# First batch's attention in 64x64 tiles, and one lying layout for keys, queries and values of batches 0 and 1

## The chip, the cores and the metric

The kernel runs on one core of a Trainium2 chip. Five engines work side by side, each through its own row of instructions in order: TensorE (PE; its weight loads PEld apart), VectorE (DVE), ScalarE (ACT), GpSimd (POOL) and SyncE (SP). They wait for each other through semaphores. Sixteen DMA engines move data; POOL and SP issue the transfers. The metric is the device time of one execution in microseconds (us); lower is better.

## What is computed

Longformer attention (a window of 32 to both sides and 8 global positions) over 8 batches of 8 heads, 576 positions and 64 dimensions, and behind it a two-layer product with a snake activation on the 4608 rows of 512.

```python
scores = scale * np.matmul(q, k.transpose(0, 1, 3, 2))
mask = np.abs(pos[:, None] - pos[None, :]) <= window
mask = mask | is_global[:, None] | is_global[None, :]
attn = softmax(where(mask, scores, -1e9))
x = (attn @ v) as rows of 512           # 4608 x 512
h = x @ w_in                             # 512 x 2048
s = np.sin(alpha * h)
out = (h + s * s / (alpha + 1e-09)) @ w_out
```

## The kernel before

The loop runs over batches. For batch b the phase *attention(b)* makes scores, masks, denominators and numerators for four head pairs (hp) and leaves xT, the normalised result, transposed. *gemm1(b)* multiplies xT by w_in in 16 groups (nt) of 128 columns: eight matmuls, a sine on ScalarE (sb), its square on ScalarE or VectorE (s), and one operation on VectorE that writes H2. *gemm2(b)* multiplies H2 by w_out in blocks of 128 rows, 16 matmuls of 512 columns each. It is not a phase of its own: it waits as a generator, and `fill(n)` puts n of its matmuls where the author of the order set them (START, FIRST, SECOND, PER_GROUP), in attention(b+1) and gemm1(b+1). So in the first attention and first gemm1 nothing can be filled in; `warm(z, n)` issues n matmuls without use there. The order of instructions on each engine is the order of the code: nothing is scheduled, and an engine in front of a wait holds all behind it.

Positions are dealt in 12 tiles of 48 keys, even and odd positions apart (y = 0 and 1), and 8 global keys follow each tile. For batches 1 to 7 scores come in 64x64 tiles: head t of a pair on partitions t\*64 and on, and two key tiles (the two halves of the sequence) share one score tile of 128 partitions by 2\*360 columns. The first batch has a function of its own, `attention_first`: it keeps keys and values of a pair block-diagonal in KD and VD, 128x128, so that these must be cleared first, and its score tile is 128x480. Its mask MASK lies by tiles, and is moved to MASKT by DMA for the batches behind it.

Set-up: POOL loads keys and queries of batch 0 in four pieces of 288 KB (each half of the heads of k, then of q), casting to bf16. TensorE transposes them (L625), and ScalarE and VectorE copy them from PSUM into KD and QX (L641, L646), the first half ahead of the attention and the second in it (`second_half`). Values of batch 0 come in 16 loads of runs of 64 elements, 128 bytes in bf16 (L397). Batch 1's values are cast into DRAM (L343, vd) and read back by SP (L418, VX). Batch 1's keys and queries are loaded lying (48 rows of 3072) and turned by TensorE in three thirds within gemm1(0) (L733, placed by L741 and L747). SP gathers the rows of the 8 global positions of all batches, eight small transfers each for k, q and v (L518); `turn_kq` transposes them in gemm1(0) at group 4 (L773, then the casts L777 to kTg and qTg).

From batch 2 on keys and queries are cast into DRAM (kd, qd) by POOL and transposed by DMA from there (kt, qt, L353, on SP, `turn_qk`); `place` copies them into KX and QX on VectorE in eight pieces (L369, L362). Values are cast into DRAM (vd) and read in four transfers on SP (`load_v`, L418). POOL's casts are paced: before batch 2's cast of values POOL waits for qt of batch 2 (`pace`, L347).

## Time and profile before

| | us |
|---|---|
| runs, median (lowest to highest of 3) | 351.45 (350.79 to 351.58) |
| profiled execution | 351.02 |
| its span in the trace | 349.2 |
| TensorE busy in the span | 314.1 (90%) |
| VectorE busy | 274.7 (79%) |
| ScalarE busy | 285.7 (82%) |
| first scores of batch 0 | 16.04 |
| first sine of batch 0 | 36.12 |
| first scores of batch 1 | 59.92 |
| first sine of batch 1 | 78.13 |
| first scores of batch 2 | 98.75 |

How to read it: a line of the timeline has the start and the length in us, the engine, the line of the program, the operation, what it writes and reads, and in brackets how long its engine was idle before and what ended that. Lengths of neighbours overlap a little, since the engines are pipelined; the distance of two starts is what one takes of the engine. The stretch from the first scores of one batch to those of the next is one round; after batch 2 the rounds repeat.

### The profile page before, as it was taken

The page shows a single profiled execution, that of the slowest core. Times are in us where ns is not written, and L with a number is a line of the kernel's source. Part 1 is how long each engine was busy: PE and PEld are TensorE (multiplying, and loading weights), DVE is VectorE, ACT ScalarE, POOL GpSimd, SP SyncE. Part 2 cuts the span into 40 slices and gives each one's busy share as a digit, 9 for nine tenths or more (in the row PEclk, how much of TensorE's full clock was granted, in tenths as well). Part 3 has the DMA queues.
Part 4 walks back from the last instruction along what each step waited for, and adds up shares of the span by engine and source line. Part 5 has one row for each costly group of instructions (what it writes and reads, how often), then busy time and mean ns, then how long its engine had stood idle before and what let it go on. Part 6 is the DMA issues. An engine that isn't in the chain of part 4 may idle for free.

```text
span 349.2 us, 10913 instructions
## 1 busy us (share of the span) xinstructions
PE 314.1 (90%) x4425; PEld 206.7 (59%) x4484; DVE 274.7 (79%) x537; ACT 285.7 (82%) x428; POOL 60.9 (17%) x93
## 2 busy tenths in 40 slices
PE   1578799899899999999999999999989999999994
PEld 1557576466655675567656765577557755665543
DVE  6786778878879788887798787978797788788940
ACT  6797688898988888989898889989898888888721
POOL 7966130023004000400012000400000000002600
PEclk9999899999999999999999999999999999999999
DMA  7999999689997948399529962791824111010232
GB/s 114 110 132 159 184 212 232 116 155 187 190 171 140 196 71 190 76 204 150 108 65 188 200 107 64 152 191 45 171 65 95 30 33 66 3 30 2 76 92 67
DMA packets 87762, 42.25 MB, mean 121 GB/s; under 512 B 72378, under 2 KB 82362, under 8 KB 87322
## 3 DMA queue, kind: packets, MB, share of 16 engines
q0 software_dynamic: 44944, 18.52, 44.1%
q1 hardware_dynamic: 42762, 22.98, 30.7%
q8 instruction: 36, 0.59, 0.8%
q14 instruction: 20, 0.16, 0.2%
HBM read 41.97 MB, written 20.77 MB: 180 GB/s over the span
## 4 chain that ended last, share of the span: by engine, by line
PE 67%; DMA 6%; DVE 5%; issue 4%; ACT 2%; SPq 1%; POOL 0%; DVEq 0%; ACTq 0%
PE zo L1270 30%; PE zn L1176 12%; PE zr L1176 9%; PE zd L1176 8%; PE ring L976 3%; DMA vd<-in_v_dram 3%; PE zn L1014 2%; DVE H L1221 2%; PE zd L1014 2%; DMA VD<-vd 2%; DMA qt<-qd 2%; DVE QX L362 2%; SPq L353 1%; PE zd L1314 1%; PE zd L1270 1%
## 5 line engine op out<-in xcount | busy, mean ns | idle before, releaser
L1270 PE MATMUL zo<-w_out,H 128*128 128x512 bf16 (+1 forms) x517 | 134.1, 376 | 5.9 <-issue 5.2
L1176 PEld LDWEIGHTS <-w_in 128*128 128x128 bf16 x1024 | 100.3, 98 | 48.6 <-issue 13.2
L1270 PEld LDWEIGHTS <-H 128*128 128x128 bf16 x592 | 53.6, 98 | 45.8 <-DMA VX<-vd 0.3
L1176 PE MATMUL zn<-xT,w_in 128*128 128x288 bf16 (+1 forms) x384 | 57.0, 287 | 5.7 <-DVE GN L801 2.7
L1176 PE MATMUL zr<-xT,w_in 128*128 128x288 bf16 x320 | 48.7, 291 | 1.2 <-DVE H L1221 1.2
L1176 PE MATMUL zd<-xT,w_in 128*128 128x288 bf16 x320 | 46.9, 290 | 0.2
L1221 DVE SCALAR_TENSOR_TENSOR H<-s,recipT,zn 128x576 bf16<-128x576 bf16 (+1 forms) x48 | 39.4, 821 | 9.1 <-ACT s L1218 5.7
L1215 ACT ACTIVATE sb<-zn,alphaT 128x576 bf16<-128x576 f32 (+1 forms) x48 | 35.6, 742 | 12.4 <-PE zn L1176 12.1
L1218 ACT ACTIVATE s<-sb 128x576 bf16<-128x576 bf16 (+1 forms) x58 | 40.0, 689 | 1.8
L1221 DVE SCALAR_TENSOR_TENSOR H<-s,recipT,zd 128x576 bf16<-128x576 bf16 (+1 forms) x40 | 32.9, 822 | 9.3 <-ACT s L1218 6.5
L1220 DVE TENSOR_TENSOR s<-sb 128x576 bf16<-128x576 bf16 (+1 forms) x70 | 32.1, 459 | 10.0 <-ACT sb L1215 9.8
L985 ACT ACTIVATE E<-ring 128x720 bf16<-128x720 f32 x42 | 32.8, 781 | 7.5 <-PE ring L976 6.8
L1221 DVE SCALAR_TENSOR_TENSOR H<-s,recipT,zr 128x576 bf16<-128x576 bf16 (+1 forms) x40 | 32.9, 822 | 6.2 <-ACT s L1218 4.6
L1215 ACT ACTIVATE sb<-zr,alphaT 128x576 bf16<-128x576 f32 (+1 forms) x40 | 29.7, 742 | 7.6 <-PE zr L1176 7.6
L986 DVE TENSOR_TENSOR E<-E,MASKT 128x720 bf16<-128x720 bf16 x56 | 29.4, 529 | 8.0 <-ACT E L985 6.3
L1215 ACT ACTIVATE sb<-zd,alphaT 128x576 bf16<-128x576 f32 (+1 forms) x40 | 29.5, 738 | 5.8 <-PE zd L1176 5.7
L1277 ACT COPY osb<-zo 128x512 f32<-128x512 f32 (+1 forms) x36 | 20.9, 581 | 10.7 <-PE zo L1270 7.0
L824 ACT ACTIVATE R<-L,shift 128x576 f32<-128x576 f32 x32 | 25.1, 784 | 0.5
L1260 POOL COPY H<-H 128x11 bf16 (+1 forms) x16 | 7.2, 452 | 98.7 <-DVE H L1221 97.9
L347 POOL COPY seen<-xT 1x1 bf16<-1x1 bf16 x4 | 1.9, 479 | 125.5 <-DVE GN L801 125.5
L1035 DVE TENSOR_TENSOR xT<-zn,R 128x576 bf16<-128x576 f32 x21 | 15.8, 753 | 1.1 <-PE zn L1014 0.9
L343 POOL DMA_DIRECT2D vd<-in_v_dram x7 | 16.3, 2333 | 0.1
(187 smaller groups left out, 376.9 us busy)
## 6 DMA issues: line engine op xcount, KB each, us to landing
vd<-in_v_dram POOLq DMA_DIRECT2D x7, 576.0 KB, 16.3
kd<-in_k_dram POOLq DMA_DIRECT2D x6, 576.0 KB, 8.2
qd<-in_q_dram POOLq DMA_DIRECT2D x6, 576.0 KB, 10.0
VX<-vd SPq DMA_DIRECT2D x16, 168.0 KB
w_in<-in_moe_w_in_dram POOLq DMA_DIRECT2D x4, 512.0 KB, 9.2
w_out<-in_moe_w_out_dram POOLq DMA_DIRECT2D x4, 512.0 KB, 24.4
VD<-vd SPq DMA_DIRECT2D x12, 168.0 KB
out_dram<-osb SPq DMA_DIRECT2D x7, 256.0 KB
```

What stands on the lines that cost most here:

```text
L343: nc.gpsimd.dma_start(out=cast[b, "vd"][:], in_=v[b].rearrange("h s d -> s h d"))
L824: nc.scalar.activation(out=R[:], in_=L[:], func=AF.Exp, scale=-1.0, bias=shift[:, 0:1])
L985: nc.scalar.activation(out=Eg, in_=z[:, :, 0 : G3 * WCOL], func=AF.Exp, scale=scale)
L986: nc.vector.tensor_tensor(out=Eg, in0=Eg, in1=MASKT[:, None, G3 * g : G3 * (g + 1), :].rearrange("p o m c -> p o (m c)").to_broadcast([P, ...
L1035: nc.vector.tensor_tensor(out=xT[:, hp, 0:S].rearrange("p (k m c) -> p k m c", k=4, c=KT), in0=tokens(nd(hp, 0)), in1=Rs[hp][:], op=ALU.mult,)
L1176: nc.tensor.matmul(out=h_part, lhsT=w_in[:, c, nt * P : (nt + 1) * P], rhs=xT[:, c, lo:hi], start=(c == 0), stop=(c == CT - 1), skip_group ...
L1215: nc.scalar.activation(out=sb[:, 0:W], in_=h, func=AF.Sin, scale=alphaT[:, nt : nt + 1])
L1218: nc.scalar.activation(out=s2[:, 0:W], in_=sb[:, 0:W], func=AF.Square)
L1220: nc.vector.tensor_tensor(out=s2[:, 0:W], in0=sb[:, 0:W], in1=sb[:, 0:W], op=ALU.mult)
L1221: nc.vector.scalar_tensor_tensor(out=H2[:, nt, r0 : r0 + W], in0=s2[:, 0:W], scalar=recipT[:, nt : nt + 1], in1=h, op0=ALU.mult, op1=ALU.add,)
L1270: nc.tensor.matmul(out=ops[:, cols], lhsT=H2[:, nt, blk * P : (blk + 1) * P], rhs=w_out[:, nt, cols], start=(nt == 0), stop=(nt == NT - 1) ...
L1277: nc.scalar.copy(out=osb[:, cols], in_=ops[:, cols])
```

## The change

`attention_first` goes. Batch 0 runs through the same function as the others, in 64x64 tiles; where there is nothing to fill in, `warm` puts two or three matmuls a head pair. KD, VD, OB and MASK go with their clearing, and the mask is made in MASKT at once.

Keys and queries of batches 0 and 1 are loaded in one lying layout, in pieces by head parity (t), all of k ahead of all of q. `turn_lying` and `place_lying` turn and place them: batch 0 wholly in the set-up, in 192 transposes instead of 96 and in copies of 128 partitions; batch 1 in gemm1(0), at groups 4, 7 and 10 instead of 2, 6 and 9. Values of batches 0 and 1 are loaded by pairs of neighbouring positions, in runs of 128 elements (256 bytes in bf16) into VF; VectorE then moves the odd rows to partitions 32 further on (`odd_rows`) and copies the two tiles at the border of the halves (`edge_tiles`, VE). Batch 1's values thus don't go through DRAM any more. Global values of batch 0 are repeated through a small DRAM tile (vgd).

Other places: the order of the loads on POOL and of the gathers on SP; `turn_kq` at group 12 of gemm1(0), behind that group's matmuls; the turn of batch 2's keys and queries behind attention(1) instead of at its second head pair; their placing wholly in gemm1(1); gemm2(0) takes the first eight groups of two blocks first.

```diff
-    def load_v0(hps):
-        for hp in hps:
-            for t in range(2):
-                for y in range(2):
-                    r = t * D + y * 24
-                    nc.gpsimd.dma_start(
-                        out=VD[r : r + 24, hp, :, t * D : t * D + D],
-                        in_=v[0, 2 * hp + t].rearrange("(i a y) d -> y a i d", a=24, y=2)[y],
-                    )
+    def load_v_lying(b, hs):
+        for h in hs:
+            for half in range(2):
+                nc.gpsimd.dma_start(
+                    out=VF[b][half * D : half * D + NH, :, h].rearrange("p m y d -> p m (y d)"),
+                    in_=v[b, h].rearrange("(n m a y) d -> n a m (y d)", n=2, a=NH, y=2)[half],
+                )
+    def odd_rows(b, hs, copy):
+        for half in range(2):
+            r = half * D
+            copy(out=VF[b][r + 32 : r + 32 + NH, :, hs, 0], in_=VF[b][r : r + NH, :, hs, 1])
+    def edge_tiles(b, hs, copy):
+        for half in range(2):
+            r, m = (1 - half) * D, half * (NT6 - 1)
+            for y in range(2):
+                o = half * D + y * 32
+                copy(out=VE[b][o : o + NH, hs], in_=VF[b][r : r + NH, m, hs, y])
...
-    load_v0((0,))
+    load_v_lying(0, range(0, 4))
     load_w_in((0,))
-    load_v0((1, 2))
+    load_v_lying(0, range(4, 8))
     load_w_in((1,))
-    load_v0((3,))
-    load_lying(0)
     load_lying(1)
     load_w_in((2, 3))
-    cast_v(1)
-    load_w_out()
+    load_w_out((0, 1))
+    load_v_lying(1, range(H))
+    load_w_out((2, 3))
+    gather(k, gk, range(3))
+    bounce_vg0()
+    gather(k, gk, range(3, 6))
     load_vg0()
+    gather(k, gk, range(6, NG))
     gather(q, gq)
+    gather(v, gv)
...
+    def turn_lying(b, w, third, z):
+        rows = slice(D * w, D * w + NI)
+        for r in range(R16):
+            for t in range(2):
+                nc.tensor.transpose(
+                    out=z[t * D : (t + 1) * D, r * NI : (r + 1) * NI], in_=lie[b][rows, t, third * R16 + r],
+                    identity=identb[rows, rows],
+                )
+    for w in (1, 0):
+        for third in range(3):
+            turn_lying(0, w, third, lain[w][third])
...
+    warm(idle, 5)
...
-        if b == 0:
-            return attention_first(beside)
...
-            fill(SECOND[hp])
+            spare_or(SECOND[hp] if b else 2)
...
+    TURNED, PLACED, GLOBALS = (4, 7, 10), (5, 8, 11), 12
-            if b == 1 and nt in (10, 12):
-                for which, t, y in PLACES[nt - 6 : nt - 4]:
+            if b == 1 and nt in (3, 6, 9, 12):
+                for which, t, y in PLACES[2 * nt // 3 - 2 : 2 * nt // 3]:
                     place(2, which, t, y, nc.vector.tensor_copy)
-            if b == 0 and nt == 4:
-                turn_kq()
...
+            if b == 0 and nt == GLOBALS:
+                turn_kq()
...
+            if b_att < 2 and at in ((0, 2) if b_att == 0 else (0,)):
+                hs = slice(at * H // 4, H // 2 + at * H // 4) if b_att == 0 else slice(0, H)
+                odd_rows(b_att, hs, nc.vector.tensor_copy)
+                edge_tiles(b_att, hs, nc.vector.tensor_copy)
...
-            if b_moe == 0 and at == 1:
+            if b_moe == 0 and at == NHP:
                 turn_qk(2)
```

How instructions move, at two places. VectorE in the first attention, before: masks of the first head pair (E, MASK), then the queries of the second half (QX), then the second pair.

```order
L851 TENSOR_TENSOR E<-E,MASK 128x480 x3
L646 COPY QX_95<-zo_124 64x2x6x2x12 x4
L646 COPY QX_95<-zo_125 64x2x6x2x12 x4
L851 TENSOR_TENSOR E<-E,MASK 128x480 x3
L801 TENSOR_REDUCE GD<-zd 128x2x4
```

The same place after; VF holds the values, VE the edge tiles.

```order
L862 TENSOR_TENSOR E<-E,MASKT 128x2x360 x2
L402 COPY VF_91<-VF_91 24x6x4x64 x2
L409 COPY VE_93<-VF_91 24x256 x4
L862 TENSOR_TENSOR E<-E,MASKT 128x2x360 x2
L794 TENSOR_REDUCE GD<-zd 128x2x4
```

The copies of queries have left the attention, and copies of values stand where they stood (and once more behind the masks of the third pair).

SP from the second head pair of batch 1's attention on, before: kt and qt are the DMA transposes of batch 2, LC stores logarithms, out_dram stores output blocks.

```order
L819 DMA LC<-L 2x576
L353 DMA_TRANSPOSE kt<-kd 128x2304
L353 DMA_TRANSPOSE qt<-qd 128x2304
L819 DMA LC<-L 2x576
L1303 DMA out_dram<-osb 16x512
L1303 DMA out_dram<-osb 112x512
L819 DMA LC<-L 2x576 x2
L1303 DMA out_dram<-osb 32x512
L1303 DMA out_dram<-osb 96x512
L418 DMA VD<-vd 24x7x512 x4
```

And after, from the second output block on:

```order
L1170 DMA out_dram<-osb 112x512
L812 DMA LC<-L 2x576 x2
L1170 DMA out_dram<-osb 32x512
L1170 DMA out_dram<-osb 96x512
L352 DMA_TRANSPOSE kt<-kd 128x2304
L352 DMA_TRANSPOSE qt<-qd 128x2304
L440 DMA VF_91<-vd 24x7x512 x4
```

The two transposes stand behind the stores of the third block, and directly ahead of the reads of batch 2's values.

More of the change, by code (lines that the diff above doesn't have):

```diff
@@ L432, in load_w_in, with load_w_out @@
             )
[L434 to L435 removed]
+    def load_w_out(gs):
+        for g in gs:
             nc.gpsimd.dma_start(
@@ L614 @@
     )
     small = tc.alloc_tile_pool(name="small", bufs=1, space=PSUM)
-    both = small.tile([P, 512], DT.float32, name="pg")
+    both, idle = [small.tile([P, 512], DT.float32, name=name) for name in ("pg", "idle")]
     act, dve = nc.scalar.copy, nc.vector.tensor_copy
-    part = {}
-    def turn_part(w, half, z):
-        part[w, half] = z
-        rows = slice(D * half, D * half + HK)
-        for a in range(NH):
-            nc.tensor.transpose(
-                out=z[a // 12][:, a % 12], in_=nat[w][rows, a * P : (a + 1) * P], identity=identb[rows, rows]
-            )
@@ L1281, in gemm2 @@
         full = slice(0, DM)
-        if b == B - 1:
-            for blk in (lo, lo + 1):
-                yield from products(blk, bank(blk), range(SOON), full)
+        ahead = {0: NT // 2, B - 1: SOON}.get(b, 0)
+        for blk in (lo, lo + 1):
+            yield from products(blk, bank(blk), range(ahead), full)
         for blk in range(lo, hi):
```

475 lines of the change are left out of this document (167 added, 308 removed).

## The prediction

> **What bounds the kernel now.** I read the span by stages first. The columns are the stretch, its length, the busy time of TensorE, its weight loads, VectorE, ScalarE and GpSimd with their instructions, the granted clock, the DMA share and GB/s. The stages: first attention, first matrix product of batch 0, attention of batch 1, first product of batch 1.
>
> ```profile
> 16.04:36.12 20.08, 16.20 (x182) 13.38 (x182) 15.09 (x44) 16.09 (x29) 13.88 (x19) 1.00 1.22 151
> 36.12:59.92 23.80, 20.66 (x320) 14.43 (x318) 17.74 (x27) 18.49 (x30) 4.08 (x7) 0.93 1.43 213
> 59.92:78.13 18.21, 16.84 (x394) 10.27 (x399) 14.25 (x30) 16.30 (x25) 2.12 (x3) 1.00 0.78 141
> 78.13:98.75 20.62, 18.61 (x130) 12.58 (x130) 18.00 (x30) 17.40 (x27) 3.53 (x4) 1.00 1.50 181
> ```
>
> From 60 us on TensorE is busy 90% or more, because a second product always has matmuls to put in a gap. Before that no engine is full: in the first two rows TensorE, VectorE and ScalarE are each busy three quarters of the time and wait in turn. The change can only win in these 44 us; what follows 98.75 keeps its order. So the sum runs to the first scores of batch 2, at 98.75. The timeline of the set-up and first attention says why its engines wait.
>
> ```profile
> 3.23 0.52 POOL L473 DMA_DIRECT2D H<-in_q_dram  x1
> 6.42 1.14 PE L625 MATMUL zn<-identb,H 48*128 48x48 bf16 x24 [6.42 <-DMA H<-in_k_dram]
> 16.04 0.96 PE L843 MATMUL ring<-QX,KD 128*128 128x120 bf16 x8 [1.17 <-ACT alphaT L709]
> 18.38 3.21 ACT L641 COPY KD<-zn 64x288 bf16<-64x288 bf16 x8
> 18.95 3.74 DVE L646 COPY QX<-zo 64x288 bf16<-64x288 bf16 x8
> 22.23 0.56 PE L843 MATMUL ring<-QX,KD 128*128 128x120 bf16 x4 [2.00 <-ACT E L850]
> 24.52 0.63 PE L576 MATMUL zo<-ones 128*128 128x512 bf16 x1
> 28.82 0.38 PE L576 MATMUL zo<-ones 128*128 128x512 bf16 x1
> 36.12 0.74 ACT L1215 ACTIVATE sb<-zn,alphaT 128x576 bf16<-128x576 f32 x1
> H<-in_q_dram POOLq DMA_DIRECT2D x1, 288.0 KB, 8.7
> ```
>
> ScalarE and VectorE spend 3.21 and 3.74 us inside the attention on the second half of keys and queries, and TensorE waits 2.00 for it. The same 512-column matmul takes 0.63 at 24.5 and 0.38 at 28.8: TensorE runs at a lower speed until about 28 us. The next stage holds one stall.
>
> ```profile
> 37.22 0.70 PE L733 MATMUL zo<-identb,H 48*64 48x48 bf16 x64
> 40.25 0.95 DVE L741 COPY KX<-zo 128x768 bf16<-128x768 bf16 x1
> 41.25 0.96 PE L773 MATMUL zo<-idf,H 64*128 64x64 f32 x8 [1.78 <-DVE KX L741]
> 42.15 2.10 PE L1176 MATMUL zr<-xT,w_in 128*128 128x288 bf16 x8
> 42.25 0.42 DVE L777 CAST kTg<-zo 128x256 bf16<-128x256 f32 x1 [0.33 <-PE zo L773]
> 44.28 0.74 ACT L1215 ACTIVATE sb<-zr,alphaT 128x576 bf16<-128x576 f32 x1 [3.32 <-PE zr L1176]
> 42.00:43.00 1.00, 1.00 (x6) 0.61 (x6) 0.75 (x2) 0.00 (x0) 0.00 (x0) 0.50 2.38 172
> ```
>
> The transposes of the global rows (L773) wait for a key copy, TensorE idles 1.78, its clock falls to 0.50, and ScalarE idles 3.32.
>
> **Term 1: the first scores, 16.04 to 17.5 (+1.5).** The loads are still four of 288 KB, but each turn now takes both pieces of its tensor, and the queries come last: the fourth load, issued at 3.23, lands 8.7 later, at 11.9. Then 96 query transposes stand on TensorE. Bounds: 0.70/64 = 11 ns each, over four quarters of the array (1.05 us), and 1.14/24 = 48 ns each (4.6). I take 30 ns (2.9), nearer to L625, which runs at this place and speed. Five warming matmuls follow, 0.38 to 0.63 each: 1.9 to 3.2, I take 2.5. With 0.2 for the global rows that makes 17.5; the bounds give 15.1 to 19.9. The copies on ScalarE and VectorE lie beside this. The memsets and clears that go saved no wait: the loads ended last.
>
> **Term 2: the first attention, 20.1 to 15.2 (-4.9).** The shapes are now those of batch 1.
>
> ```profile
> 59.92 0.35 PE L976 MATMUL ring<-QX,KX 64*64 64x88 bf16 x14
> 61.25 0.77 ACT L985 ACTIVATE E<-ring 128x720 bf16<-128x720 f32 x1
> 62.05 1.20 DVE L986 TENSOR_TENSOR E<-E,MASKT 128x720 bf16<-128x720 bf16 x2 [0.55 <-ACT E L985]
> 65.31 0.68 ACT L817 ACTIVATE L<-zd 128x576 f32<-128x576 f32 x1
> 66.03 0.23 DVE L801 TENSOR_REDUCE GD<-zd 128x8 f32<-128x64 f32 x1 [0.62 <-ACT L L817]
> 66.51 0.81 ACT L824 ACTIVATE R<-L,shift 128x576 f32<-128x576 f32 x1
> 68.26 0.75 DVE L1035 TENSOR_TENSOR xT<-zn,R 128x576 bf16<-128x576 f32 x1
> 68.38 0.49 PE L1014 MATMUL zd<-E,ones 56*64 56x88 bf16 x28
> 73.96 0.91 DVE L369 COPY KD<-kt 64x1152 bf16<-64x1152 bf16 x2
> 77.29 1.91 DVE L369 COPY KD<-kt 64x1152 bf16<-64x1152 bf16 x2
> ```
>
> ScalarE: eight exponentials at 0.77, four logarithms at 0.68, four inverses at 0.81: 12.1. VectorE: eight masks at 0.60, four normalisations at 0.75, eight sums at 0.23: 9.6. New on VectorE are four copies of odd rows (1536 elements a partition) and eight of edge tiles (256). The trace has no such copy; the nearest is 1152 elements in 0.455. In proportion that is 0.61 and 0.10; with a fixed part an edge copy is at most 0.455. I take 0.6 and 0.2: 4.0 in all (3.2 to 6.0). VectorE thus has 13.6 and becomes the longest; with 1.1 ahead of the first mask (0.35 + 0.77) and 0.5 behind the last, 15.2. ScalarE's 12.1 alone would give 13.7. The copies wait for values: eight loads of four heads, needed about 20, and for these the DMA rows count.
>
> ```profile
> VD<-in_v_dram POOLq DMA_DIRECT2D x4, 36.0 KB, 3.5
> 11.00:12.00 1.00, 0.00 (x0) 0.00 (x0) 0.97 (x3) 0.96 (x4) 1.00 (x2) 1.00 1.00 73
> 36.00:37.00 1.00, 1.00 (x10) 0.78 (x8) 0.10 (x1) 0.99 (x3) 0.05 (x1) 1.00 1.27 201
> ```
>
> While 128-byte runs move (11 us) the engines carry 73 GB/s, against 201 with long ones, and are full either way. Runs twice as long should land the 36 KB loads no later than 3.5 us after issue; the values are there by 17 or 18, and I cost this at nothing. The cast of batch 1's values through DRAM, and its reading back, go as well, which frees the engines for later loads.
>
> In VectorE's row of instructions (shown with the change) the query copies went ahead of the attention, and the copies of values took their place between the masks of the first two head pairs.
>
> **Term 3: first product of batch 0, 23.8 to 21.4 (-2.4).** The turn of the global rows moves from group 4 to behind group 12, one group further from the key copy whose bank it takes. The 3.32 stall goes; the two casts of 0.42 on VectorE, which it hid, now count: -3.3 + 0.9. Bounds: -3.3 and -0.5 (the stall returns in part).
>
> **Term 4: attention of batch 1, +2.0.** At its first head pair VectorE gets two odd-row copies of 3072 elements and four edge copies of 512: 1.2 and 0.2 each, 3.2, and loses the 0.91 pair. Behind them stand the square of xT and the masks of the second pair, which TensorE's denominators wait for. VectorE idles 4.0 in this stage (18.21 less 14.25), so part is absorbed: 0.3 to 3.2, I take 2.0.
>
> **Term 5: first product of batch 1, +1.5.** All eight copies for batch 2 now stand here instead of four: two pairs more, 0.91 each (1.91 as at 77.29). On SP the two transposes of batch 2 move from the second head pair to the end of the attention (the SP rows shown with the change). They now stand behind the stores of the third output block, and POOL's cast of batch 2's values waits for them.
>
> ```profile
> 70.19 5.71 DMA qt<-qd
> 78.26 0.79 SPq L1303 DMA_DIRECT2D out_dram<-osb  x2
> 82.16 0.81 DVE L1221 SCALAR_TENSOR_TENSOR H<-s,recipT,zd 128x576 bf16<-128x576 bf16 x1 [0.46 <-PE zn L1176]
> 93.90 6.67 SPq L353 DMA_TRANSPOSE kt<-kd  x1
> 132.31 2.10 SPq L353 DMA_TRANSPOSE kt<-kd  x1
> ```
>
> Counted from the first sine (78.13), the transpose can be issued at 0.9 and lands 4 to 5.7 later; VectorE reaches the first copy after group 2, at 4.8. So a wait of 0 to 1.8. VectorE idles 2.6 there and takes up some: 0 to 4, I take 1.5.
>
> **Sum.** 1.5 - 4.9 - 2.4 + 2.0 + 1.5 = -2.3. The profiled execution took 351.02 (span 349.2 and 1.8 around it): 348.7. The median of the runs is 0.43 above it: **349.1**. The runs spread by 0.2%, so within 0.2% (0.7 us) counts as no change.
>
> **Rivals.**
> *Half clock (0.20): 351.4.* TensorE's work in the new first attention is short: eight score groups at 0.35, eight products at 0.49, ten warming matmuls at 0.38: 10.5 of 15.2, with gaps. The trace had 1.78 us idle and then 0.50. At half clock that is 21. Bounds of the loss: 0, if all of it fits beside VectorE, and 21 less 15.2, 5.8. I take 2.3, below the middle, since listed matmuls overlap. The Trainium skill (TensorE: Matmul & The Clock Gate, Part 1) gives about 3.4 us of idleness for the fall; by that rule the gaps here are too short, and the forecast stands. The 0.50 behind 1.78 us speaks for the row.
> *Batch 2 comes late (0.18): 354.0.* Slower. If the transpose takes 6.67 on SP as at 93.90, keys land at 0.9 + 6.7 + 3.6 (5.71 less the 2.10 of a quick issue) = 11.2 after the first sine, 6.4 after VectorE wants them, and everything behind waits: -2.3 + 6.4 is 4.1, less the 1.5 already in term 5, 2.6 over the median. It decides from a landing 7 after the sine on. For it: just one group of room. Against: 2.10 when the queue is empty, which the paced cast makes it.
> *Copies blocked (0.08): 352.5.* The pair at 77.29 took 1.91 instead of 0.91. Two lost 1.0 there. If the 18 new copies lost 0.3 each, that is 5.4, of which I let VectorE's idle time take 2.0: 3.4 worse than the sum. The row
>
> ```profile
> 108.28 1.38 DVE L369 COPY KX<-kt 64x1152 bf16<-64x1152 bf16 x3
> ```
>
> shows three unstretched. The Trainium skill (SBUF — State Buffer, Who interferes with whom) has such copies and GpSimd exclude each other; POOL issues loads through this whole attention, which speaks against the change.
> *All absorbed (0.12): 345.7.* Terms 4 and 5 cost nothing: -5.8.
>
> **Numbers.** The forecast has 0.42; its own range, by the term bounds taken halfway, is 347 to 351. The range of all cases is 345.7 to 354.0. Faster: 0.39 + 0.12 + 0.09 of half clock = 0.60. Slower: 0.01 + 0.06 + 0.18 + 0.07 = 0.32. The rest, 0.08, is the same.
>
> **What would show it.** Right: first scores near 17.5 and first sine near 32.7; no idle sine above 1 us in batch 0's product; scores of batch 1 near 54, of batch 2 near 96.5. Wrong: 512-column matmuls of 0.63 in the first attention; key copies of batch 2 that wait for kt; odd-row copies well over 0.6 or waiting for a load; first scores after 19.

## The result, and the profile after

The change made the kernel slower: 366.7 us median (366.0 to 366.9, four runs) against 351.3 beside it, ratio 1.0436 (95% interval 1.0418 to 1.0455). The forecast was 349.1. The profiled execution has a span of 364.3, 15.1 more than before.

The stages show where. The view is the prediction's (stretch, length, busy time of TensorE, its weight loads, VectorE, ScalarE, GpSimd, clock, DMA share, GB/s), cut at the first scores and the first sine of each batch. The rows are the first attention, the first product of batch 0, then attention and product of batch 1, then of batch 2.

```profile
19.12:37.58 18.46, 14.27 (x362) 9.55 (x363) 12.83 (x32) 12.27 (x17) 9.98 (x16) 0.82 1.17 172
37.58:59.70 22.12, 20.05 (x321) 14.82 (x318) 19.01 (x28) 19.15 (x31) 13.39 (x22) 1.00 1.03 141
59.70:83.60 23.90, 19.21 (x400) 10.83 (x400) 15.17 (x31) 15.74 (x24) 0.54 (x2) 0.93 0.48 104
83.60:108.52 24.92, 19.03 (x131) 12.47 (x129) 20.46 (x32) 17.45 (x27) 5.67 (x5) 1.00 1.04 150
108.52:131.04 22.52, 18.48 (x396) 10.48 (x396) 15.34 (x33) 15.75 (x24) 3.68 (x4) 0.92 1.43 193
131.04:150.68 19.64, 19.64 (x141) 13.40 (x140) 15.74 (x25) 16.76 (x25) 0.00 (x0) 1.00 0.70 112
```

Batch 2's attention in the kernel before:

```profile
98.75:116.04 17.29, 15.88 (x390) 9.73 (x396) 15.15 (x33) 15.73 (x24) 3.79 (x4) 1.00 0.91 162
```

At 59.70 the kernel is level with the one before (59.92): the first two stages won 3.3, and the first scores came 3.1 later (19.12 for 16.04). Then three stages lose: batch 1's attention 5.7 (23.90 for 18.21), its product 4.3 (24.92 for 20.62), batch 2's attention 5.2 (22.52 for 17.29). They make 15.2; the product of batch 2 takes 19.64 as before. No engine is busy through any of the three (TensorE 19.21 of 23.90, VectorE 20.46 of 24.92, TensorE 18.48 of 22.52), so most of the loss is waiting; in the two attentions TensorE also works longer than before (19.21 for 16.84, 18.48 for 15.88) at granted clocks of 0.93 and 0.92. First, GpSimd's queue ahead of batch 1's attention, and SyncE's load of its global values (row SPq):

```profile
26.48 1.10 POOL L490 DMA_DIRECT2D H<-in_k_dram  x2 [1.61 <-DMA VF<-in_v_dram]
27.56 1.09 POOL L490 DMA_DIRECT2D H<-in_q_dram  x2
28.61 1.58 POOL L459 DMA_DIRECT2D w_in<-in_moe_w_in_dram  x2
30.15 0.77 POOL L465 DMA_DIRECT2D w_out<-in_moe_w_out_dram  x1
31.27 0.74 POOL L465 DMA_DIRECT2D w_out<-in_moe_w_out_dram  x1 [0.34 <-DMA w_in<-in_moe_w_in_dram]
34.15 0.63 POOL L394 DMA_DIRECT2D VF<-in_v_dram  x1 [2.14 <-DMA H<-in_k_dram]
...
44.07 0.60 POOL L394 DMA_DIRECT2D VF<-in_v_dram  x1 [2.67 <-DMA w_in<-in_moe_w_in_dram]
46.73 0.60 POOL L394 DMA_DIRECT2D VF<-in_v_dram  x1 [2.06 <-DMA w_out<-in_moe_w_out_dram]
...
54.55 1.54 POOL L465 DMA_DIRECT2D w_out<-in_moe_w_out_dram  x2
58.71 1.34 SPq L427 DMA_DIRECT2D VF<-VGe  x2
59.19 0.55 POOL L335 DMA_DIRECT2D kd<-in_k_dram  x1
```

Count back from 34.15: the load waits for the first key load at 26.48, eight issues earlier. So it goes on: each transfer that GpSimd issues waits for the landing of the one eight issues before, whatever its size. Of the 16 small loads of batch 1's values, seven come out between 34.15 and 46.73, mostly one by one, and nine in a row from 49.23 to 54.5; everything behind them is late: the last two w_out loads start at 54.55 (the last one before: 37.19), the casts of batch 2 at 59.19 (before: 48.80). TensorE pays in batch 1's attention:

```profile
62.64 0.38 PE L1137 MATMUL zo<-w_out,H 128*128 128x512 bf16 x1 [0.37 <-DMA w_out<-in_moe_w_out_dram]
66.30 1.24 PE L1137 MATMUL zo<-w_out,H 128*128 128x512 bf16 x5 [1.76 <-DMA w_out<-in_moe_w_out_dram]
69.64 0.23 PE L890 MATMUL zn<-E,VF 56*64 56x88 bf16 x2 [1.82 <-DMA VF<-VGe]
70.61 0.76 PE L890 MATMUL zn<-E,VF 56*64 56x88 bf16 x22 [0.74 <-DMA VF<-VGe]
71.32 2.31 PE L1137 MATMUL zo<-w_out,H 128*128 128x512 bf16 x5
```

These are 4.69 of waiting, and then five matmuls in 2.31 that took 1.24 at 66.30: the clock had fallen. Next, the rows of SyncE, VectorE, GpSimd and TensorE that follow the moved transposes of batch 2:

```profile
84.61 2.55 SPq L352 DMA_TRANSPOSE kt<-kd  x1
89.99 0.92 DVE L368 COPY KX<-kt 64x1152 bf16<-64x1152 bf16 x2 [1.86 <-DMA kt<-kd]
92.06 0.18 POOL L346 COPY seen<-qt 1x1 bf16<-1x1 bf16 x1 [31.82 <-DMA qt<-qd]
93.49 2.24 POOL L342 DMA_DIRECT2D vd<-in_v_dram  x1 [1.25 <-issue]
93.81 2.71 DVE L368 COPY KX<-kt 64x1152 bf16<-64x1152 bf16 x2
97.98 1.14 PE L1061 MATMUL zn<-xT,w_in 128*128 128x288 bf16 x8 [2.33 <-DVE H L1106]
109.48 5.99 SPq L352 DMA_TRANSPOSE kt<-kd  x1
121.05 1.40 DVE L368 COPY KX<-kt 64x1152 bf16<-64x1152 bf16 x3 [2.92 <-DMA kt<-kd]
121.33 0.72 PE L890 MATMUL zn<-E,VF 56*64 56x88 bf16 x27 [3.53 <-issue]
```

The keys land 5.4 after their issue and VectorE waits 1.86. The landing of the queries releases GpSimd's casts (92.06, before: 75.94), which now fall on the second pair of key copies: 2.71 instead of 0.92. From there the delay goes on to batch 3: SyncE waits 11.8 us for the cast of batch 2's values and reads them at 102.11 (before: 85.53), and the first transpose of batch 3, eight of SyncE's issues behind the first of these reads, waits 2.4 us for that read to land. So it is issued inside batch 2's attention (109.48, before: 93.90, ahead of it), and VectorE waits there again. The cast of batch 3's keys is not what it waits for: that landed at 105.6. TensorE itself stands for 3.53 us in this stage (121.33), and for some 3.4 us behind that the granted clock is 0.50; what may hold TensorE there is told in the last section.

### The profile page after: what moved, and what is told of

Same layout as the page of the kernel before. It is cut to its first block, busy times and chain, and to the rows that moved or that the text cites. A ratio compares the mean times of both kernels' runs of the same rounds, so it can differ in the third digit from the quotient of the medians.

```text
span 364.3 us, 11522 instructions
## 1 busy us (share of the span) xinstructions
PE 325.4 (89%) x4767; PEld 206.4 (57%) x4767; DVE 276.4 (76%) x537; ACT 276.0 (76%) x406; POOL 68.3 (19%) x110
## 3 DMA queue, kind: packets, MB, share of 16 engines
q0 software_dynamic: 40128, 18.52, 40.6%
## 4 chain that ended last, share of the span: by engine, by line
PE 64%; DMA 19%; DVE 4%; POOL 4%; ACT 4%; issue 3%; SPq 0%; POOLq 0%; ACTq 0%; DVEq 0%
PE zo L1137 29%; PE zn L1061 11%; PE zr L1061 8%; PE zd L1061 8%; DMA w_out<-in_moe_w_out_dram 5%; DMA w_in<-in_moe_w_in_dram 4%; DMA qt<-qd 3%; DMA VF<-VGe 3%; DMA H<-in_q_dram 3%; PE ring L852 3%; POOL VF L394 2%; PE zn L890 2%; DMA kt<-kd 1%; PE zd L890 1%; ACT sb L1100 1%
## 5 line engine op out<-in xcount | busy, mean ns | idle before, releaser
L1137 PE MATMUL zo<-w_out,H 128*128 128x512 bf16 (+1 forms) x576 | 149.6, 381 | 2.1 <-DMA w_out<-in_moe_w_out_dram 2.1
L861 ACT ACTIVATE E<-ring 128x720 bf16<-128x720 f32 x48 | 37.3, 778 | 23.8 <-PE ring L852 23.1
L1061 PE MATMUL zr<-xT,w_in 128*128 128x288 bf16 x320 | 47.7, 287 | 0.1
L862 DVE TENSOR_TENSOR E<-E,MASKT 128x720 bf16<-128x720 bf16 x64 | 33.6, 529 | 15.0 <-ACT E L861 13.1
L852 PEld LDWEIGHTS <-KX 64*64 64x64 bf16 x896 | 15.3, 112 | 23.2 <-issue 21.8
L394 POOL DMA_DIRECT2D VF<-in_v_dram x32 | 19.3, 622 | 16.4 <-DMA w_in<-in_moe_w_in_dram 6.7
## 6 DMA issues: line engine op xcount, KB each, us to landing
w_in<-in_moe_w_in_dram POOLq DMA_DIRECT2D x4, 512.0 KB, 11.9
```

Source lines behind the costliest of these rows:

```text
L394: nc.gpsimd.dma_start(out=VF[b][half * D : half * D + NH, :, h].rearrange("p m y d -> p m (y d)"), in_=v[b, h].rearrange("(n m a y) d -> n ...
L852: nc.tensor.matmul(out=z[half * D : (half + 1) * D, t, 0 : G3 * WCOL].rearrange("p (m x c) -> p m x c", x=2, c=60)[:, m % G3, :, c0:c1], l ...
L861: nc.scalar.activation(out=Eg, in_=z[:, :, 0 : G3 * WCOL], func=AF.Exp, scale=scale)
L862: nc.vector.tensor_tensor(out=Eg, in0=Eg, in1=MASKT[:, None, G3 * g : G3 * (g + 1), :].rearrange("p o m c -> p o (m c)").to_broadcast([P, ...
L1061: nc.tensor.matmul(out=h_part, lhsT=w_in[:, c, nt * P : (nt + 1) * P], rhs=xT[:, c, lo:hi], start=(c == 0), stop=(c == CT - 1), skip_group ...
L1137: nc.tensor.matmul(out=ops[:, cols], lhsT=H2[:, nt, blk * P : (blk + 1) * P], rhs=w_out[:, nt, cols], start=(nt == 0), stop=(nt == NT - 1) ...
```

## The experiments

Three theories stood against each other at the start: Q (GpSimd's queue), S (the moved transposes) and C (the half clock); the expectations say what each means.

Stage lengths in us of every profiled run, read from the timelines, and the ratio to the kernel before beside it. The stages are of the one profiled run and the ratio of all, so the two need not agree to the microsecond:

| kernel | first scores | attention 0 | product 0 | attention 1 | product 1 | attention 2 | ratio |
|---|---|---|---|---|---|---|---|
| before | 16.04 | 20.08 | 23.80 | 18.21 | 20.62 | 17.29 | 1 |
| after | 19.12 | 18.46 | 22.12 | 23.90 | 24.92 | 22.52 | 1.0436 |
| e1 | 18.97 | 19.45 | 22.73 | 17.14 | 25.32 | 23.75 | 1.0361 |
| e2 | 18.96 | 17.92 | 22.09 | 25.89 | 21.40 | 17.28 | 1.0222 |
| e3 | 18.67 | 22.10 | 22.18 | 17.16 | 21.04 | 17.28 | 1.0064 |
| e4 | 15.96 | 19.67 | 22.07 | 20.66 | 24.28 | 23.30 | 1.0273 |
| e5 | 17.54 | 18.80 | 22.56 | 17.11 | 21.04 | 17.28 | 0.998 |
| e6 | 18.32 | 16.48 | 22.90 | 23.93 | 21.04 | 17.29 | 1.0137 |
| e7 | 18.73 | 17.69 | 24.50 | 18.94 | 21.05 | 20.65 | 1.0104 |
| e8 | 16.07 | 19.61 | 24.68 | 17.61 | 35.98 | 17.28 | 1.0483 |
| e9 | 18.42 | 16.11 | 22.79 | 25.15 | 21.03 | 17.28 | 1.0158 |
| e10 | 18.45 | 15.45 | 22.26 | 25.36 | 21.04 | 17.28 | 1.015 |
| e11 | 18.52 | 16.73 | 22.76 | 23.46 | 21.04 | 17.29 | 1.0135 |
| e12 | 18.27 | 17.68 | 22.80 | 17.27 | 21.59 | 17.39 | 1.0118 |
| e13 | 18.82 | 17.26 | 23.25 | 17.29 | 21.82 | 17.28 | 0.9993 |
| e14 | 17.95 | 16.38 | 23.12 | 17.53 | 21.77 | 17.30 | 1.0057 |

**e1: batch 1's values by DRAM again.**

```
-    load_w_out((0, 1))
-    load_v_lying(1, range(H))
-    load_w_out((2, 3))
+    cast_v(1)
+    load_w_out(range(4))
...
+            if b == 0 and nt == 6:
+                cast_globals_v()
+                load_vg(1)
+                load_v(1)
```

> The changed kernel with batch 1's values back on their old way: one cast to DRAM on GpSimd's queue in place of 16 loads, read back by SyncE; the cast of the global values back at group 6; no odd-row and edge copies in batch 1's attention. Everything else as in the changed kernel.
> Theory Q (each of GpSimd's DMA instructions waits for the landing of the one eight issues before it, so the 16 loads hold back the last two w_out loads and the global values): the waits of attention 1 go (w_out 0.37 and 1.76, global values 1.82 and 0.74), also 3.1 us of copies; first sine of batch 1 comes about 5.7 us earlier against the first scores of batch 1, and the time is 360 to 362. The late transposes of batch 2 remain: 4.3 us in batch 1's product and 5.2 us in batch 2's attention.
> Theory S (the transposes moved behind the attention are the whole loss, the waits for w_out only fill time that would be lost anyway): 365 to 367.
> Theory C (half clock in the first attention is what costs): 366 to 367, no change, since nothing changes ahead of 37 us.

Measured 363.5, ratio 1.0361 (1.0311 to 1.0411). Attention 1 drops from 23.90 to 17.14: the queue and the copies were the whole loss there. But by the ratios only 2.6 of these 6.8 us reach the end (the interval is 1.8 wide each way), and the time is outside the 360 to 362 of theory Q. The cast now meets the edge copies in the first attention (below, e3), and the product of batch 1 and the attention of batch 2 wait longer (25.32 and 23.75): what waits for the transposes of batch 2 is still there.

**e2: the transposes of batch 2 back at the second head pair.**

```
-            if b_moe == 0 and at == NHP:
+            if b_moe == 0 and at == 1:
```

> The changed kernel with the two transposes of batch 2 back at the second head pair of batch 1's attention; all eight copies stay in batch 1's product. Nothing else differs.
> Theory S (the move costs 4.3 us in batch 1's product, where the key copies wait, and 5.2 us in batch 2's attention, since the casts of batch 3 wait for the transposes): 357 to 359.
> Theory Q (GpSimd's queue is late as a whole: batch 2's casts, issued at 59 instead of 49, land at about 75, so that the transposes now block SyncE's queue from 65 to 75 with the stores behind them): of the 9.5 us only 3 to 6 come back, 361 to 364, and the output copies wait for free buffers in batch 1's attention.
> Theory C: 366 to 367.

Measured 358.4, ratio 1.0222 (1.018 to 1.0265): theory S. Product 1 is at 21.40 and attention 2 at 17.28, 8.8 us off the two stages. Attention 1 pays 2.0 more (25.89), for SyncE, GpSimd and TensorE there read:

```profile
68.08 3.71 SPq L352 DMA_TRANSPOSE kt<-kd  x1
76.57 0.18 POOL L346 COPY seen<-qt 1x1 bf16<-1x1 bf16 x1 [16.71 <-DMA qt<-qd]
70.86 1.02 PE L890 MATMUL zn<-E,VF 56*64 56x88 bf16 x24 [5.94 <-DMA VF<-VGe]
```

The casts are released at 76.57 again, and the wait for global values (5.94) stands alone. Theory Q's fear, that late casts would hold the transposes and block SyncE until 75, came true only in small part: SyncE waited 1.1 us for the cast of the keys and issued kt at 68.08, 1.4 later than before. Theory C, no change, is ruled out by e1 and e2 alike.

**e3: both edits together.**

> The edits of the last two kernels together: batch 1's values by DRAM and the transposes of batch 2 at the second head pair. What is left of the change: first attention in 64x64 tiles, lying keys and queries of batch 0, lying values of batch 0, the new order of batch 0's product.
> If queue and move are the two causes and add up (5.7 and 9.5): 351 to 353, that is about the time before. If what is left still gains as forecast (first attention shorter, stall of batch 0's product gone): 347 to 350. If the two overlap (the casts of batch 2 are early again only here): this gains more than the two apart add up to.

Measured 352.8, ratio 1.0064 (1.0038 to 1.009): 13.0 of the 15.3 are back, more than e1 and e2 apart (2.6 and 7.5): the two losses overlap. The rest of the change costs 2.2 us, and its first attention took 22.10. Its rows:

```profile
24.57 0.28 PE L889 MATMUL zn<-E,VF 56*64 56x88 bf16 x2 [2.04 <-DMA VF<-vgd]
26.12 0.76 PE L889 MATMUL zn<-E,VF 56*64 56x88 bf16 x22 [1.27 <-DMA VF<-vgd]
28.42 1.04 PE L608 MATMUL zo<-ones 128*128 128x512 bf16 x2
30.41 2.26 POOL L342 DMA_DIRECT2D vd<-in_v_dram  x1
30.79 3.07 DVE L409 COPY VE<-VF 24x256 bf16<-24x256 bf16 x4
35.27 0.76 PE L889 MATMUL zn<-E,VF 56*64 56x88 bf16 x24 [3.19 <-DVE GN L793]
```

Two things: the global values of batch 0 land late and the clock falls (two matmuls in 1.04), and four edge copies, 0.95 at their first use in the changed kernel (its row stands in the part on why the prediction was wrong), take 3.07 beside GpSimd's cast, and TensorE waits 3.19 for VectorE behind them.

**e4: the kernel before with the moved transposes alone** (and, as in the change, all eight copies in batch 1's product).

```
-            if b_moe == 0 and at == 1:
+            if b_moe == 0 and at == NHP:
...
-            if b == 1 and nt in (10, 12):
+            if b == 1 and nt in (3, 6, 9, 12):
...
-        share = {3: (0, 2), 4: (2, 4)} if b_att == 1 else {2: (0, 3), 3: (3, 6), 4: (6, 8)}
+        share = {} if b_att == 1 else {2: (0, 3), 3: (3, 6), 4: (6, 8)}
```

> The kernel before with one part of the change alone: the transposes of batch 2 behind batch 1's attention and all eight copies in batch 1's product.
> Theory S: the move costs the same without anything else, about 9.5 us: 360 to 361.5.
> Theory Q: the move is cheap where the casts have landed long before (at about 65) and the DMA engines are free: 0 to 4 us, 351.5 to 355.
> The forecast's term 5 said 1.5, and its rival 4.1.

Measured 360.2, ratio 1.0273 (1.024 to 1.0306): 9.6 us. The move alone costs what theory S said, without any of GpSimd's small loads. All of it arises behind the first sine of batch 1, which comes at 78.36 (before: 78.13): the 2.45 more in attention 1, with 1.86 of waiting for w_out, only take back what product 0 was shorter. Its rows of VectorE are like those of the changed kernel:

```profile
85.00 0.92 DVE L369 COPY KD<-kt 64x1152 bf16<-64x1152 bf16 x2 [2.42 <-DMA kt<-kd]
88.82 1.77 DVE L369 COPY KD<-kt 64x1152 bf16<-64x1152 bf16 x2
115.88 1.39 DVE L369 COPY KX<-kt 64x1152 bf16<-64x1152 bf16 x3 [3.65 <-DMA kt<-kd]
```

**e5: the global values of batch 0 left out** (zeros in their rows; otherwise e3).

```
+    nc.vector.memset(VF[0][:].rearrange("p m h y d -> p (m h y d)"), 0.0)
...
-    bounce_vg0()
...
-    load_vg0()
```

> The kernel with both parts put back (values of batch 1 by DRAM, transposes at the second head pair), and with the global values of batch 0 left out: their rows in the value tile are zeros, so nothing waits for their two trips (to DRAM and back). This prices that wait in the first attention, which took 18.5 in the changed kernel and 22.1 in the kernel with both parts put back, against a forecast of 15.2.
> If the wait (1.46 and 1.41 in the changed kernel, 2.04 and 1.27 in the other) and the half clock that follows it (512-column matmuls at 0.51 to 0.61 until 32 us) are what failed: first attention 15 to 18, first sine at 34 to 37, time 347 to 350.
> If VectorE's copies are what failed (four edge copies took 3.07 beside GpSimd's cast): first attention 20 or more, 350.5 to 352.

Measured 349.3, ratio 0.998 (0.9966 to 0.9995). Of the 2.9 us that it gains on e3 by the ratios, all lies ahead of the first sine, which comes at 36.34 instead of 40.77 in the profiled runs (1.1 of it ahead of the first scores). The edge copies still take 2.91 beside the cast:

```profile
26.39 2.26 POOL L342 DMA_DIRECT2D vd<-in_v_dram  x1
26.77 2.91 DVE L409 COPY VE<-VF 24x256 bf16<-24x256 bf16 x4
```

**e6: global values sooner, cast of batch 1's values last.**

```
-    for name, src in (("k", k), ("q", q), ("v", v)):
+    for name, src in (("v", v), ("k", k), ("q", q)):
...
-    cast_v(1)
     load_w_out(range(4))
+    cast_v(1)
-    gather(k, gk, range(3))
     bounce_vg0()
-    gather(k, gk, range(3, 6))
     load_vg0()
-    gather(k, gk, range(6, NG))
+    gather(k, gk)
```

> The kernel with both parts put back, with two moves: the indirect gather of the global values goes ahead of those of keys and queries on GpSimd's queue and their two trips ahead of the other gathers on SyncE's; the cast of batch 1's values goes behind the four w_out loads, away from the edge copies of the second half. Nothing is left out.
> If the late global values and the stretched edge copies are the two losses of the first attention: the global values land 2 to 3 us sooner, the edge copies take 1 to 1.5 instead of 3.07, first attention 16 to 18, time 347 to 350.
> If the first scores (which wait for query transposes and global keys) come later by the gather's move: up to 1 us back.
> If the DMA engines are simply full from 18 to 26 us: the global values land no sooner and only the edge copies gain: 350 to 351.5.

Measured 355.5, ratio 1.0137 (1.0104 to 1.017): a miss as a whole. The first attention did fall to 16.48 with nothing left out, and batch 1's scores came at 57.70; but now batch 1's values, cast last, were read back by SyncE at 58.69 only, and attention 1 took 5.7 us more than before. What each of the two moves gave in the first attention, the kernel does not separate.

**e7: the lying loads kept, w_out ahead of them, global values cast on VectorE** (otherwise e2).

```
-    load_w_out((0, 1))
+    load_w_out(range(4))
     load_v_lying(1, range(H))
-    load_w_out((2, 3))
...
-        nc.gpsimd.tensor_copy(out=VGe[:], in_=gv[:, :, None, :].to_broadcast([NG * B, H, 2, D]))
+        nc.vector.tensor_copy(out=VGe[:], in_=gv[:, :, None, :].to_broadcast([NG * B, H, 2, D]))
...
+            if b == 0 and nt == 9:
+                cast_globals_v()
+                load_vg1()
```

> The changed kernel with the transposes at the second head pair, and two moves that leave its loads of batch 1's values as they are: all four w_out loads ahead of them on GpSimd's queue, and the cast of the global values of batch 1 on VectorE at group 9, not on GpSimd behind the loads. Against the kernel with the transposes alone put back (358.4).
> Theory Q (order on the queue is the cause, not the number of bytes): the wait of 5.94 for global values and the waits for w_out go, attention of batch 1 takes 19 to 21 instead of 25.9, time 351 to 354.
> Rival (16 small loads fill the DMA engines until 60 us whatever their order): values or casts of batch 2 land late instead; the odd-row copies wait, 355 to 358.

Measured 354.2, ratio 1.0104 (1.0073 to 1.0134): theory Q. Attention 1 takes 18.94 with all 16 loads in place, 1.8 more than with values by DRAM; no transfer is waited for in it, TensorE waits 0.62 and 0.93 for VectorE, and so I take the 1.8 as the price of the odd-row and edge copies. The wait did not vanish but moved to the copy of global queries, now last on GpSimd's queue:

```profile
53.84 5.32 POOL L394 DMA_DIRECT2D VF<-in_v_dram  x9 [2.05 <-DMA w_out<-in_moe_w_out_dram]
60.92 0.35 PE L851 MATMUL ring<-QX,KX 64*64 64x88 bf16 x13 [1.78 <-POOL QX L379]
```

Attention 2 took 20.65 here, 3.4 more than in e2. VectorE does not wait for kt in it; 3.2 are two TensorE stalls that the profile puts down to nothing (last section).

**e8: e4 with the casts released early.**

```
-            pace(turned[2][0][0:1, 0:1])
+            pace(xTs[1][0:1, 2, 0:1])
```

> The kernel before with the transposes moved (360.2), but with GpSimd's casts of batch 2's values and of batch 3 released by batch 1's third head pair instead of by the landing of the transposed queries: they are issued at about 74 as before.
> If the chain transposes, casts of batch 3, transposes of batch 3 is what carried the loss into batch 2's attention: that attention is back at 17 to 18 (from 23.3), batch 1's product keeps the wait for keys (2.4) but loses the stretched copies: 351.5 to 355.
> If the wait for keys in batch 1's product is the main loss: 357 to 359.

Measured 366.3, ratio 1.0483 (1.0434 to 1.0532). Both expectations missed the total, yet half of the first one holds: attention 2 is back at 17.28 with the casts released early, as it would be if their late release carried the loss into it. The run does not separate this cleanly, since its product of batch 1 is so long that the transfers for batch 3 have more time in any case; in e4 the link is seen as a wait: SyncE's first transpose of batch 3 waits 3.8 for the reads of batch 2's values. What nobody expected is the product of batch 1, 35.98:

```profile
75.47 2.23 POOL L343 DMA_DIRECT2D vd<-in_v_dram  x1
78.98 11.61 SPq L353 DMA_TRANSPOSE kt<-kd  x1
96.25 0.92 DVE L369 COPY KD<-kt 64x1152 bf16<-64x1152 bf16 x2 [14.06 <-DMA kt<-kd]
```

Transposes that start behind four casts take 11.61 on SyncE's queue instead of 2.77. Late transposes lose either way: ahead of the casts they delay batch 3, behind them they crawl. Why they crawl is not shown.

**e9 to e12: getting batch 1's values in on time.** e9 puts the cast of e6 behind the first w_out load, e10 adds six warming matmuls to e9, e11 lets SyncE gather the global values ahead of the global queries and read batch 1's values before it spreads them, e12 holds batch 2's casts in e11 until group 14.

```
e9
-    load_w_out(range(4))
+    load_w_out((0,))
     cast_v(1)
+    load_w_out((1, 2, 3))
e10
-            spare_or(SECOND[hp] if b else 2)
+            spare_or(SECOND[hp] if b else (2, 2, 2, 8)[hp])
e11
     gather(k, gk)
+    gather(v, gv)
     gather(q, gq)
-    gather(v, gv)
...
-                load_vg(1)
                 load_v(1)
+                load_vg(1)
e12
+                pace(H2[0:1, NT - 2, 0:1])
                 cast_qk(2)
```

> The kernel with the global values sooner, whose first attention took 16.5 (forecast 15.2), but with the cast of batch 1's values behind the first of the four w_out loads instead of behind the last: there it was issued at 36.5 and landed at about 58, so that SyncE read it back at 58.7 to 64 and TensorE waited 3.1 and 1.8 in batch 1's attention (23.9). Behind the first it should be issued at about 31, after the edge copies (which ended at 28.6).
> If the order on GpSimd's queue is all that was wrong there: first attention 16 to 17, batch 1's attention 17.2, batch 1's product 21.0, batch 2's attention 17.3; first scores of batch 2 at about 96, time 346.5 to 348.5, below the kernel before.
> If the cast meets the edge copies again: edge copies near 3, first attention 18 to 19, 349 to 351.
> If the three w_out loads behind the cast now come late: waits for w_out in batch 1's attention, 350 or more.

> The last kernel with eight warming matmuls instead of two behind the last head pair's scores of the first attention, where TensorE idled 2.28 and then ran the first chunks of batch 0's product at half speed (six in 1.60 instead of 0.90).
> If the half clock costs there: 0.7 to 1.5 less than the last kernel.
> If VectorE and ScalarE set the end of the first attention: no change within 0.4, or up to 0.5 more, where the warming matmuls stand ahead of the last products.

> The kernel with the cast between the w_out loads, which took 355.8: its first scores of batch 1 came at 57.3, 2.6 ahead of the kernel before, but TensorE then waited 4.67 for batch 1's values, which SyncE read back at 50.3 to 51.9 behind the global values, 4 us ahead of batch 2's casts, and which landed only at 67.5. Here SyncE gathers the global values of the other batches ahead of the global queries, and reads batch 1's values before it spreads the global ones.
> Theory D (the DMA engines are full from 15 to 65 us, so a shorter first attention only meets transfers that are not done; the order of transfers decides what is waited for): the values are read at about 45 to 48 and land before 62, and the wait goes: batch 1's attention 17 to 19, time 347.5 to 350.5. If w_out, the last in line, is then what is waited for (1 to 3 us): 350 to 352.
> If the landing depends on batch 2's casts alone and not on when it is issued: no better than 354.

> The last kernel with batch 2's casts of keys and queries held until group 14 of batch 0's product is written (about 57, where they were issued at 54).
> Theory D: what was waited for in batch 1's attention lands 1 to 3 us sooner, since the two casts (2 of 576 KB) no longer share the engines with it; the transposes of batch 2 wait on SyncE 1 to 3 us more, hidden: 347 to 349.5, or as the last kernel if nothing was waited for there.
> If the casts now come too late (transposes landing behind batch 2's first copies): 350 to 353.

Measured 355.8, 355.3, 355.2 and 355.0; ratios 1.0158, 1.015, 1.0135, 1.0118, no two apart by their intervals (about 0.4% each way). All four missed the time that they were made for. The first attention is short in the first three (16.11, 15.45, 16.73) and batch 1's attention gives it back (23.46 to 25.36). From e9:

```profile
50.27 1.60 SPq L440 DMA_DIRECT2D VF<-vd  x4
68.02 0.78 PE L888 MATMUL zn<-E,VF 56*64 56x88 bf16 x26 [4.67 <-DMA VF<-vd]
```

Values that SyncE starts to read at 50.27 are there only at 68. In e10 the extra warming made the first attention 0.66 shorter, and nothing that stands clear of the noise reached the end. e11 moved the read far less than meant (45 to 48): SyncE waited 5.9 us for the cast, which landed 18.8 us after its issue, and read at 49.85; TensorE then waited 3.18 for the global values, now behind. e12 fell into two groups, 350.2 and 351.2 against four of 354.8 to 356.3; its profiled run, one of the short ones, has no such wait (attention 1: 17.27). None of the long ones was profiled.

**e13, e14: the cast ahead of batch 1's keys and queries**, in e11 and in e12.

```
+    cast_v(1)
     load_lying(1)
     load_w_in((2, 3))
     load_w_out((0,))
-    cast_v(1)
     load_w_out((1, 2, 3))
```

> The kernel that reads batch 1's values first (355.2), with the cast of those values ahead of batch 1's lying keys and queries on GpSimd's queue: issued at about 24.5 instead of 31, ahead of the second pair of odd-row copies (26.1) and the edge copies (27.3). Its 2.2 us of issue push the lying loads, two of w_in and the w_out loads that much later.
> If the landing of batch 1's values is all that was waited for: SyncE reads them at 43 to 46, they land by 60, batch 1's attention takes 17 to 18.5, 347 to 349.5, below the kernel before.
> If transfers as a whole are late: w_out or lying keys are waited for instead; 351 to 355.

> The same, with batch 2's casts held until group 14 of batch 0's product (58.6 instead of 55).
> If batch 1's values are safe by their earlier issue, holding brings nothing: as the last kernel within 0.7.
> If transfers as a whole are late: 1 to 4 below the last kernel, and its executions no longer fall into two groups 5 us apart, as those of the kernel with the casts held and the values read first did (350.2, 351.2, and four of 354.8 to 356.3).

Measured 350.1, ratio 0.9993 (0.9968 to 1.0017), and 351.6, ratio 1.0057 (1.003 to 1.0083). SyncE reads the values at 45.78 in e13, attention 1 takes 17.29, as hoped for, and nothing in it waits for a transfer; the time is above the 347 to 349.5 that should have followed. So the landing of batch 1's values was what the short first attention had run into. Holding the casts brings nothing on top: by the ratios, whose intervals do not overlap, it costs 2 us. Why is open: the profiled run of e14 took 349.7 (all: 349.4 to 353.6) and does not show it. With these transfers in time what is left of the change gains nothing that can be measured, and no version that computes the whole result beats the kernel before (e5, at 0.998, leaves the global values out).

## Why the prediction was wrong

The sum said -2.3 and the span grew by 15.1. The 17.4 between them lie, by its terms, at 1.6 (term 1), 3.3 (term 2), 0.7 (term 3), 3.7 (term 4), 2.8 (term 5) and 5.2 behind its end. Three of the signs that I had named for being wrong appeared: a 512-column matmul of 0.61 in the first attention, key copies of batch 2 that wait for kt, and first scores after 19. (One reading was loose: in the first two stages TensorE was busy 81% and 87%, not three quarters.)

**The sum's end.** The step that failed worst is the sentence that what follows 98.75 keeps its order, "so the sum runs to the first scores of batch 2". 5.2 of the 15.2 us arose behind it, in batch 2's attention: the cast of batch 2's values, which I had waiting for the transposes, sets when SyncE reads these values, and that read sets when batch 3's transposes start. I had named that wait, and followed it no further. e4 and e2 show that the loss comes and goes with the place of the transposes, and the waits of SyncE in e4 and in the changed kernel show the chain up to the transposes of batch 3. How these cost 5.2 us is less sure: VectorE's wait for kt and TensorE's stall fall together there.

**Term 5, +1.5 forecast, +4.3 measured, and +5.2 behind it.** The two further pairs of copies were priced too high: with the transposes back product 1 takes 21.04 to 21.40, 0.4 to 0.8 over before. The wait for keys was 1.86, just over the 0 to 1.8 that I gave it. What was left out is that the casts, released later, meet the second pair (2.71 for 0.92; 1.77 in e4) and TensorE idles 2.33.

**The rival "batch 2 comes late"** named the right place and the wrong point: it decides, I wrote, from a landing 7 us after the sine. The keys landed at 6.4 (89.99 less 83.60), and the loss came all the same.

**Term 4, +2.0 forecast, +5.7 measured.** The copies were sized well: 1.93 and 1.19 in the changed kernel, where I had 2.4 and 0.8, and by e7 they cost about 1.8 in time. The failed step is the loads of batch 1's values and the order on GpSimd's queue, costed at nothing. I counted bytes and issue times there, and not the number of issues that may be under way.

**Term 2, -4.9 forecast, -1.6 measured.** VectorE's work was right (12.83 busy for 13.6), and so was the size of the copies (0.57 and 0.24 at first use for 0.6 and 0.2). The failed step is again a cost of nothing: the two trips of batch 0's global values, which the sum does not mention. Changed kernel, VectorE's first edge copies and TensorE:

```profile
22.25 0.69 PE L608 MATMUL zo<-ones 128*128 128x512 bf16 x2
22.95 0.95 DVE L409 COPY VE<-VF 24x256 bf16<-24x256 bf16 x4
24.68 0.23 PE L890 MATMUL zn<-E,VF 56*64 56x88 bf16 x2 [1.46 <-DMA VF<-vgd]
26.32 0.75 PE L890 MATMUL zn<-E,VF 56*64 56x88 bf16 x22 [1.41 <-DMA VF<-vgd]
27.03 0.61 PE L608 MATMUL zo<-ones 128*128 128x512 bf16 x1
```

The wait is 2.87, and behind it the 512-column matmul is back from 0.35 to 0.61: the rival of the half clock came true, set off by that wait. The stage also began at the lower speed, ahead of any wait (two such matmuls took 1.04 at 19.89), which the sum did not count. Where the global values come sooner and the cast of batch 1's values stands elsewhere (e6, e9, e11 to e14) the stage takes 16.1 to 17.7, and 15.45 with more warming, close to my 15.2.

The Trainium skill (TensorE: Matmul & The Clock Gate, Part 1) asks for an idle window of about 3.4 us. Here the granted clock fell at about 25.9 (0.94 in the slice from 25 to 26, 0.50 in the next, and so until 32.7), after 1.46 and about 1 us of idling with 0.23 of matmuls between, and 1.78 was enough in the kernel before; by that rule I had called the gaps too short, and the measurement decides.

**Term 1, +1.5 forecast, +3.1 measured**, inside its bounds. The query transposes took about 2.75 us (13.67 to 16.42) for the 2.9 that I took, and the five warming matmuls 2.31 for 2.5. The fourth load was mis-sized: its transposes start at 13.67, where I had it landing at 11.9.

**Term 3, -2.4 forecast, -1.7 measured.** The stall is gone as said. But e4, whose code is that of the kernel before there, took 22.07 in this stage and e8 24.68 (before: 23.80), so the 1.7 cannot be told from the spread of the stage.

**Copies blocked** (chance 0.08) holds as a mechanism. Copies stretch where they meet GpSimd's cast of values: 2.71, 3.07 and 2.91 for work of 0.92 and 0.95. The row stands; the Trainium skill (SBUF — State Buffer, Who interferes with whom) has such copies and GpSimd exclude each other, and the traces agree as far as the stretching goes.

## What to carry to other kernels

Follow a moved transfer past the next thing that waits for it, to the transfers that this releases, and do not end the sum before the last of them. Before splitting one load into many on a queue, count how many may be under way, and list what stands behind them. A stage that gets shorter meets the transfers of the next one sooner: ask for each what lands when, because the gain of the first stage was lost there in four kernels.

## What the runs showed of the hardware

A transposing load behind four casts took 11.61 us on SyncE's queue (e8), against 2.77 at the same place without them (e4). Four 168 KB reads of values took some 17 us to land (50.27 to 68 in e9). The DMA engines' share was 1.0 to 1.3 until 61, but 0.35 to 0.92 from there on, so full engines alone do not explain it. e12 fell into two groups 5 us apart; that a transfer landing near the moment when it is wanted makes the difference is my reading, and no run shows it. What a late landing does is seen in e9: behind the wait of 4.67 the clock is at 0.50, and four matmuls take 1.91 (at 69.13).

TensorE's stalls of 1 to 3.5 us inside groups of products, which the profile puts down to nothing, stand in batch 2's attention of the changed kernel, e4 and e7. The two of e7:

```profile
111.22 0.50 PE L889 MATMUL zn<-E,VF 56*64 56x88 bf16 x27 [1.03 <-issue]
117.98 0.27 PE L889 MATMUL zr<-E,ones 56*64 56x120 bf16 x9 [2.17 <-issue]
```

The DMA records have a hint. A queue of the kind "instruction" moves packets of 16 KB, 38 in the changed kernel, one for about every 250 of TensorE's recorded matmuls and weight loads. Such a packet ended at 109.87 and at 116.71 in e7, at 112.49 and 120.87 in e4 (TensorE went on at 114.09 and 122.22), and at 119.99 in the changed kernel (121.33): each of the five stalls ends 1.3 to 1.6 us behind one. Two of a kernel, in e4 and e7, lie 255 or 256 records apart. This fits TensorE waiting for its own code while the DMA engines are busy, in the changed kernel with the transposes (share 1.3 to 2.5 from 117 to 120); no run here tested it. In e7 the two stalls are nearly all of the 3.4 us that the stage takes more.
